# An attention and MLP kernel that runs by a written list: the list made anew

## The chip, the cores and the metric

The kernel runs on one core of a Trainium2 chip. The metric is the device time of one execution in microseconds (us). Before the change it is 630.63 us, the median of three runs (630.5 to 630.87).

## The reference

Everything is bf16 at the edges; S = 2048 rows, D = 512, 32 heads of 16 that share one key and one value (multi-query attention), F = 1792.

```
xn  = layernorm(x)
q   = (xn @ wq) per head;  k = xn @ wk;  v = xn @ wv
p   = softmax(q k^T / 4);  s = (p v, heads side by side) @ wo
g   = silu( silu(xn @ w1) @ w2 )
out = x + s * g
```

The 32 heads x 2048 x 2048 exponentials are the bulk of the work: 134 million of them.

## The kernel before

**Tiling.** The rows are cut into 4 chunks of 512 queries (`NQ`), the keys into 16 tiles of 128, the heads into 8 groups of 4. A *block* is one head, one key tile and one query chunk: 128 keys x 512 queries of scores, 2048 blocks in all. A *group* (32 of them, `gi`) is four heads of one chunk. TensorE makes a block's scores with a matmul of 32 rows of contraction in one of four row strips (`score`, L672); four strips run side by side. The products with V (`emit_quad`, L798) run in four column strips: four matmuls side by side are called a *quad*. Dense work (the MLP's two layers, the q projections and the output projection) runs in quads too (L433).

**Two ways to take an exponential.** ScalarE takes the exponential of two blocks at once from a psA buffer (two of 1024 columns, `exp_A`, L703) into one of 11 slots of `pa_sb`. VectorE takes a block from psD, psF or psO by adding a bias and writing int16, whose bits are a bf16 that approximates the exponential (`exp_D`, L743); two blocks that lie side by side in psD can be taken by one instruction of 1024 columns, a *pair*. GpSimd adds two constants to the finished four blocks of a key tile (`shift`, L768, `INT64_ADD`), so three weighted versions are summed by V's products: a VectorE block costs three V matmuls, a ScalarE block one. The versions lie in `ph_sb`, or in a part of `x_sb` that is free by then.

**Banks.** psA holds ScalarE's scores, psD two of VectorE's blocks, psF one dense job or a block, and psO the V products of the group that is open. At a group's end VectorE transposes psO (L911), later takes reciprocals (L920), normalises (L901, a `TENSOR_TENSOR` with two inputs in SBUF) and transposes back (L937). Only after the first transposition may the next group's V products begin. A *dense job* accumulates in a bank; ScalarE then takes a tanh (L1145) and VectorE the last step of silu (L1164), or VectorE alone evicts it (L1171, L1176).

**What sets the order.** After some 30 us, when the layer norm and the first projections are done, `follow` reads a string, `ORDER`, letter by letter, and issues each engine's instructions in that order; `finish` does the same with `TAIL`. Every engine then works in its own order, and waits are placed where data or banks demand them. The letters that matter here:

- `R0`/`R1`: a burst of two score blocks into psA; `e`: their exponential on ScalarE; `H`: such a burst of the last group's four first key tiles, which are done in three parts of the queries
- `o..` opens a key tile for VectorE, `f..` makes one of its blocks in a bank (0 and 1 psD, 2 psF, 3 psO), `x` evicts one block, `y` a pair
- `v`: one quad of V's products. Which blocks it takes (those that are ready first) is decided by a cost model of the engines in class `Sched`, which keeps estimated times for that purpose
- `J..b` opens a dense job in bank b, `d3` issues three of its quads, `t` its tanh, `E.` its eviction
- `1` to `4`: the four steps at a group's end
- in `TAIL`: `q`: V products of a part, `n`: a step of the part's normalisation, `P` and `r`: quads of the last output projection, `C`, `M`, `G`: evictions by ScalarE, VectorE or both, `X`, `Y`, `Z`/`z`: a tile of the output summed on TensorE, copied by ScalarE and stored, `A`/`B`: summed on VectorE and stored (the two cases name the queue that stores)

In `Sched.model`, a VectorE instruction with a pair as its cost is one with two tensors in SBUF; the model delays it behind GpSimd's additions that it finds in its way.

Of the kernel before, what the change touches and what calls it, by code (L numbers as in the profile page):

```python
# [35 lines left out]
class Sched:  # L36
# [64 lines left out]
    def model(self, eng, lane, cost, r):  # L101
        if lane:
            t = max(self.free[eng], r) + 0.05
            self.free[eng] = t + (0.86 if eng == "gp" else 0.5)
            return t + (cost or 2.25)
        if eng == "pe" and self.fine:
            mode, tiles, cols = cost or ("full", [None] * 4, 128)
            t = r
            for tile in tiles:
                end = self.pe_last + self.pe_len  # L110
                if mode != self.pe_mode:
                    t = max(t, end + (0.098 if mode == "row" else 0.1012))
                    self.pe_tiles, self.pe_pos = set(), 0
                elif tile is not None and tile not in self.pe_tiles:
                    t = max(t, self.pe_last + 0.0033)
                else:
                    self.pe_pos += 1
                    t = max(t, end + (0.003 if mode != "col" or self.pe_pos == 1 else -0.0075))
                    self.pe_tiles = set()
                self.pe_tiles.add(tile)  # L120
                self.pe_mode, self.pe_last, self.pe_len = mode, t, max(cols, 60) / 2400.0
            self.free[eng] = t
            return t + cols / 2400.0 + 0.2125
        if eng == "pe":
            mode, tiles, cols = cost or ("full", [None] * 4, 128)
            t = r
            for tile in tiles:
                if mode != self.pe_mode:
                    t = max(t, self.pe_last + self.pe_len + self.SWITCH)
                    self.pe_tiles = set()  # L130
                elif tile is not None and tile not in self.pe_tiles:
                    t = max(t, self.pe_last + 0.004)
                else:
                    t = max(t, self.pe_last + self.pe_len + 0.003)
                    self.pe_tiles = set()
                self.pe_tiles.add(tile)
                self.pe_mode, self.pe_last, self.pe_len = mode, t, max(cols, 60) / 2400.0
                self.pe_runs.append((t, t + self.pe_len))
            self.free[eng] = t
            return t + cols / 2400.0 + self.FLY + self.SEM  # L140
        if eng == "a" and self.fine:
            n = cost or 512
            t = max(r, self.free["a"], self.act_end - 0.428)
            self.free["a"] = t
            self.act_end = max(t + 0.1707 + n / 1200.0, self.act_end + 0.0632 + n / 1200.0)
            return self.act_end + 0.055
        if eng == "a":
            n = cost or 512
            t = max(r, self.free["a"], self.act_end - 0.428)
            self.free["a"] = t  # L150
            self.act_end = max(t + 0.274 + n / 1200.0, self.act_end + 0.0635 + n / 1200.0)
            return self.act_end + self.SEM
        t = max(r, self.free[eng] - (0.084 if eng == "v" else 0.0))
        if eng == "v" and isinstance(cost, tuple):

            t = max(r, self.free[eng] - 0.13)
            end = t + cost[0]
            for a, b in self.gp_runs[-6:]:
                if a < t - 0.1:
                    end = max(end, b + cost[0] - 0.13)  # L160
            self.tt_runs.append((t, end))
            self.free[eng] = end
            return end + (0.0565 if self.fine else self.SEM)
        end = t + (cost or 0.4)
        if eng == "gp" and cost and cost > 1.0:
            for a, b in self.tt_runs[-3:]:
                if a <= t + 0.1 and b > t:
                    end = max(end, b + 0.89)
            self.gp_runs.append((t, end))
        self.free[eng] = end - (0.02 if self.fine and eng == "gp" else 0.0)  # L170
        return end + (0.0565 if self.fine else self.SEM)
# [71 lines left out]
def bass_recurrent_scan__grouped_kv_mqa__dense_activation_silu__prompt_kernel(  # L243
# [76 lines left out]
        a=(0.3, 3.0, 0.65, 10, 1.2, 2.0, -4, 24, 0.2, 3, 3, 0.04, 9, 0.43, 0, 0.33, 0, 0),  # L320
# [7 lines left out]
    TAIL = "vvHvvHPvvvvvvvHHq0q0q0q0q1q1q1q1n0PPn1n0n1PPPq2q2q2n0n1n0q2PPr0r1n2C1n1n2n2G0Pr2Pn2PG2Pr3C3X1M1Y1A2A0M3Z1A3"  # L328
    ALPHA = "".join(chr(x) for x in range(35, 127) if x != 92) + "".join(chr(x) for x in range(192, 255))

    with ExitStack() as es:
# [1206 lines left out]
        while not followed:  # L1538
# [3 lines left out]
            if not followed and settled():  # L1542
# [3 lines left out]
                K.fine = True  # L1546
                follow(ORDER)
                followed = True
                continue
            t = max(now, min(K.pe_next("col"), K.pe_next("full")))  # L1550
# [14 lines left out]
            if more:  # L1565
# [4 lines left out]
                if TWIN and K.pe_mode == "row" and not front and release() <= K.pe_next("row") + 0.12:  # L1570
                    slots, t = 0, K.pe_next("row")
# [39 lines left out]
            else:  # L1611
                now = 0.0
        finish(TAIL)
        last = {}
# [36 lines left out]
```

## Time and profile before

| | |
|---|---|
| median of three runs | 630.63 us |
| the profiled execution: its own time / its span | 631.2 / 629.4 us |
| granted TensorE clock | 1.000 |
| ScalarE: exponentials of 128 x 1024 / tanh | 622 / 72 |
| VectorE: evictions of 512 / of 1024 columns (L743) | 708 / 48 |
| GpSimd: additions of 128 x 1024 (L768) | 402 |

The span runs from the first to the last instruction; the execution's own time is 1.8 us longer. In the groups of the page a mean duration counts from an instruction's start to its end, and instructions of one engine overlap a little, so the time from start to start is shorter than the mean. In a timeline, neighbours of one kind are merged into a row with their count. A `[0.23 <-PE psA L721]` behind a row is the idle time ahead of it and what ended that.

### The profile page before, as it was taken

How to read it: one execution, taken by the hardware profiler on the slowest of the kernel's cores; microseconds unless marked ns; L12 is line 12 of the kernel's file. 1: busy time of each engine (PE TensorE's matmuls, PEld its weight loads, DVE VectorE, ACT ScalarE, POOL GpSimd, SP SyncE). 2: the span in 40 equal slices, each digit the busy share in tenths (PEclk: the TensorE clock that was granted, in tenths of full speed). 3: DMA queues.
4: the chain of work that ended last, by engine and by line, in shares of the span. 5: the costliest groups of instructions: out<-in, count | busy, mean ns of one | idle time of the engine just before them, and what ended most of it. 6: DMA issues, size and time to landing. Idle time of an engine off the chain costs nothing.

```text
span 629.4 us, 18825 instructions
## 1 busy us (share of the span) xinstructions
PE 621.7 (99%) x8257; PEld 199.6 (32%) x8259; DVE 612.0 (97%) x1017; ACT 618.9 (98%) x714; POOL 443.5 (70%) x446
## 2 busy tenths in 40 slices
PE   8999999999999999999999999999999999999997
PEld 3422333333233333333332333323333233333333
DVE  7999999999999999999999999999999999999994
ACT  7999999999999999999999999999999999999996
POOL 5477665676766788676687767678775776787763
PEclk9999999999999999999999999999999999999999
DMA  6380000000000010000000000001000000000002
GB/s 178 126 287 1 2 2 2 2 1 3 1 3 2 2 18 11 10 2 2 1 3 2 1 3 1 2 11 18 10 2 2 2 2 1 2 3 1 11 11 51
DMA packets 10082, 12.50 MB, mean 20 GB/s; under 512 B 2288, under 2 KB 9456, under 8 KB 9968
## 3 DMA queue, kind: packets, MB, share of 16 engines
q1 hardware_dynamic: 7840, 9.34, 4.5%
q0 software_dynamic: 1728, 1.57, 2.2%
q8 instruction: 64, 1.05, 0.7%
q10 hardware_dynamic: 432, 0.39, 0.2%
q14 instruction: 18, 0.15, 0.1%
HBM read 8.95 MB, written 4.19 MB: 21 GB/s over the span
## 4 chain that ended last, share of the span: by engine, by line
PE 72%; ACT 24%; DVE 2%; DMA 1%; issue 0%; SPq 0%
PE psO L798 28%; PE psA L672 22%; ACT pa_sb L703 22%; PE psF L433 17%; PE psD L672 2%; ACT t_sb L1145 2%; DMA x_sb<-in_A_x_dram 1%; DVE ph_sb L743 0%; PE psF L672 0%; PE psD L536 0%; PE psD L505 0%; PE psA L721 0%; PE psD L562 0%; ACT xnT_sb L526 0%; DVE onb_sb L901 0%
## 5 line engine op out<-in xcount | busy, mean ns | idle before, releaser
L703 ACT ACTIVATE pa_sb<-psA 128x1024 bf16<-128x1024 f32 x622 | 583.5, 1058 | 2.5 <-PE psA L721 1.3
L768 POOL INT64_ADD ph_sb<-ph_sb x302 | 314.0, 1060 | 118.7 <-DVE ph_sb L743 118.3
L743 DVE TENSOR_SCALAR ph_sb<-psD 128x512 int16<-128x512 f32 (+1 forms) x462 | 320.6, 723 | 4.4 <-PE psD L672 3.5
L798 PE MATMUL psO<-ph_sb,vaug_sb 128*32 128x512 bf16 x1812 | 229.1, 384 | 0.0
L798 PE MATMUL psO<-pa_sb,vaug_sb 128*32 128x512 bf16 (+2 forms) x1276 | 205.5, 379 | 0.2 <-ACT pa_sb L703 0.2
L768 POOL INT64_ADD x_sb<-x_sb x100 | 104.1, 1057 | 41.6 <-DVE x_sb L743 41.4
L672 PE MATMUL psA<-qT_sb,kTb_sb 32*128 32x512 bf16 x616 | 118.8, 384 | 0.2 <-ACT pa_sb L703 0.2
L672 PE MATMUL psA<-qT_sb,kTa_sb 32*128 32x512 bf16 x612 | 116.5, 384 | 0.2
L672 PE MATMUL psD<-qT_sb,kTa_sb 32*128 32x512 bf16 x350 | 107.1, 384 | 0.5 <-DVE x_sb L743 0.5
L743 DVE TENSOR_SCALAR x_sb<-psD 128x512 int16<-128x512 f32 (+1 forms) x152 | 106.0, 717 | 0.9 <-PE psD L672 0.6
L798 PE MATMUL psO<-x_sb,vaug_sb 128*32 128x512 bf16 x600 | 105.1, 383 | 0.0
L672 PE MATMUL psD<-qT_sb,kTb_sb 32*128 32x512 bf16 x312 | 95.3, 384 | 0.0
L798 PEld LDWEIGHTS psO<-ph_sb,vaug_sb 128*32 128x32 bf16 x1812 | 59.1, 95 | 57.5 <-issue 34.2
L433 PE MATMUL psF<-w_sb,u_sb 128*32 128x512 bf16 x896 | 67.0, 383 | 0.0
L798 PEld LDWEIGHTS psO<-pa_sb,vaug_sb 128*32 128x32 bf16 x1276 | 52.5, 94 | 42.7 <-issue 31.1
L433 PE MATMUL psF<-xnT_sb,w_sb 128*32 128x512 bf16 x896 | 64.2, 382 | 0.0
L672 PEld LDWEIGHTS psA<-qT_sb,kTb_sb 32*128 32x128 bf16 x616 | 28.9, 91 | 109.3 <-ACT pa_sb L703 93.2
L672 PEld LDWEIGHTS psA<-qT_sb,kTa_sb 32*128 32x128 bf16 x612 | 28.7, 91 | 104.7 <-ACT pa_sb L703 78.5
L743 DVE TENSOR_SCALAR ph_sb<-psF 128x512 int16<-128x512 f32 x80 | 54.5, 681 | 0.1
L1145 ACT ACTIVATE t_sb<-psF 128x512 bf16<-128x512 f32 x72 | 45.2, 627 | 0.2 <-PE psF L433 0.2
L1164 DVE SCALAR_TENSOR_TENSOR u_sb<-t_sb,psF 128x512 bf16<-128x512 bf16 x56 | 37.9, 677 | 0.0
L798 PEld LDWEIGHTS psO<-x_sb,vaug_sb 128*32 128x32 bf16 x600 | 26.6, 95 | 20.1 <-issue 11.5
(120 smaller groups left out, 423.2 us busy)
## 6 DMA issues: line engine op xcount, KB each, us to landing
w_sb<-in_B_w_dram SPq DMA_DIRECT2D x2, 1792.0 KB, 12.1
x_sb<-in_A_x_dram SPq DMA_DIRECT2D x3, 512.0 KB, 5.8
out_dram<-ob_sb POOLq DMA_DIRECT2D x12, 128.0 KB, 3.1
wop_sb<-in_A_wo_dram SPq DMA_DIRECT2D x1, 512.0 KB, 4.4
wq_sb<-in_A_wq_dram SPq DMA_DIRECT2D x1, 384.0 KB, 5.8
out_dram<-ob_sb SPq DMA_DIRECT2D x3, 128.0 KB, 1.7
x_sb<-in_A_x_dram SPq DMA_DIRECT2D x2, 128.0 KB, 2.9
x_sb<-in_A_x_dram ACTq DMA_DIRECT2D x2, 128.0 KB, 3.1
```

Source lines behind the costliest of these rows:

```text
L433: r = e.matmul(bank[32 * i:32 * i + 32, :], lhsT=w, rhs=rhs, start=start, stop=stop, tile_position=(0, 32 * i), skip_group_check=True)
L672: return e.matmul(ap, lhsT=kT_sb[g % 2][32 * i:32 * i + 32, kt * P:(kt + 1) * P], rhs=qT_sb[32 * i:32 * i + 32, c % 2, g // 2, :], start=T ...
L703: d = op("a", lambda e: e.activation(pa_sb[:, sl, :], psA[k][:, :], ACT.Exp, scale=ESCALE), reads=["A%d" % k], writes=[("pa", sl)], cost=2 ...
L743: d = op("v", lambda e: e.tensor_scalar(ph_ap(0, sl, 512 * pos, 512 * pos + m), src, float(PH_ONE + PH_BIAS), 0.0, op0=ALU.add, op1=ALU.ma ...
L768: d = op("gp", lambda e, j=j: e.int64_add(ph_ap(j, sl, 0, 4 * NQ).bitcast(I64), ph_ap(0, sl, 0, 4 * NQ).bitcast(I64), PH_SHIFT[j] * 0x0001 ...
L798: r = e.matmul(psO[32 * i:32 * i + 32, cs], lhsT=vaug_sb[:, p["v"], p["kt"], DH * (gi % 2):DH * (gi % 2) + 32], rhs=p["ap"], start=s0, sto ...
L1145: d = op("a", lambda e: e.activation(t_sb[:, n % 2, :], bank_ap(b), ACT.Tanh, scale=0.5 if jb[0] == "h" else 0.25), reads=[b], writes=[("t ...
L1164: op("v", lambda e: e.scalar_tensor_tensor(out=dst, in0=t_sb[:, n % 2, :], scalar=1.0, in1=src, op0=ALU.add, op1=ALU.mult), reads=tk["read ...
```

## The change

The program's functions stay. `ORDER` and `TAIL` are replaced, and one line of the model that helps choose each quad's blocks:

```diff
@@ class Sched, model(): a VectorE instruction with two tensors @@
             for a, b in self.gp_runs[-6:]:
-                if a < t - 0.1:
+                if a < t + (0.15 if self.fine else -0.1):
                     end = max(end, b + cost[0] - 0.13)
...
-    ORDER = "R0xf11f01exJ$2d2R1xf10exd2R0E$o02f03evvR1xf10ev
...
+    ORDER = "R0xf11xf00eJ$2d3R1xf11xevd1R0E$o02f02evR1xf11eJ
...
-    TAIL = "vvHvvHPvvvvvvvHHq0q0q0q0q1q1q1q1n0PPn1n0n1PPPq2q2q2n0n1n0q2PPr0r1n2C1n1n2n2G0Pr2Pn2PG2Pr3C3X1M1Y1A2A0M3Z1A3"
+    TAIL = "q0vvHvHvvq0q0q0vvHHn0Pq1n0q1n0n0q1q1Pn1PPPr0n1n1Pr1q2q2q2q2G0PPPn2C1n1r2Pn2PM1n2A1C2Pn2r3X2B0M2G3Y2z2B3"
```

What the new list holds, counted letter by letter against the old one:

| | before | after |
|---|---|---|
| bursts into psA in `ORDER` (`R` and `H`) | 597 | 595 |
| key tiles for VectorE opened in `ORDER` | 199 | 200 |
| their evictions: single (`x`) / pairs (`y`) | 704 / 48 | 580 / 112 |
| V quads in `ORDER` / in `TAIL` (`v`) | 892 / 11 | 898 / 7 |
| dense jobs in psF / in psO | 99 / 0 | 77 / 22 |
| all exponentials on ScalarE | 622 | 620 |
| all additions on GpSimd | 402 | 404 |

**TensorE at the end of the second group.** Before: V's products (L798) of the group end, and a job of the MLP's first layer (`w_sb`, L433) follows in psF, then the next group's products. psA and psD rows are score bursts.

```order
L798 MATMUL psO<-pa_sb,vaug_sb 32x512 x2
L798 MATMUL psO<-ph_sb,vaug_sb 32x512 x6
L672 MATMUL psA<-qT_sb,kTa_sb 128x512 x2
L672 MATMUL psD<-qT_sb,kTa_sb 128x512
L433 MATMUL psF<-xnT_sb,w_sb 32x512 x16
L672 MATMUL psA<-qT_sb,kTa_sb 128x512 x2
L672 MATMUL psD<-qT_sb,kTa_sb 128x512
L798 MATMUL psO<-x_sb,vaug_sb 32x512 x2
L798 MATMUL psO<-pa_sb,vaug_sb 32x512
```

After:

```order
L798 MATMUL psO<-pa_sb,vaug_sb 32x512 x2
L798 MATMUL psO<-ph_sb,vaug_sb 32x512 x4
L798 MATMUL psO<-pa_sb,vaug_sb 32x512 x2
L433 MATMUL psF<-xnT_sb,w_sb 32x512 x4
L672 MATMUL psA<-qT_sb,kTa_sb 128x512 x2
L672 MATMUL psD<-qT_sb,kTa_sb 128x512 x2
L433 MATMUL psF<-xnT_sb,w_sb 32x512 x12
L672 MATMUL psA<-qT_sb,kTa_sb 128x512 x2
L433 MATMUL psO<-xnT_sb,w_sb 32x512 x16
L672 MATMUL psA<-qT_sb,kTa_sb 128x512 x2
L672 MATMUL psD<-qT_sb,kTa_sb 128x512 x2
L433 MATMUL psF<-xnT_sb,w_sb 32x512 x16
```

Here the next group's V products are put off; job after job runs in turn in psF and psO, six of them at this place, a job to nearly every burst.

**VectorE near the last group's beginning.** Evictions of scores (L743) ahead of the transposition that ends the group before the last. Before:

```order
L743 TENSOR_SCALAR ph_sb<-psF 128x512
L743 TENSOR_SCALAR ph_sb<-psD 128x512 x2
L743 TENSOR_SCALAR x_sb<-psF 128x512
L743 TENSOR_SCALAR x_sb<-psD 128x512 x2
L911 STREAM_TRANSPOSE otr_sb<-psO 128x16x32
```

After:

```order
L743 TENSOR_SCALAR ph_sb<-psD 128x1024
L743 TENSOR_SCALAR ph_sb<-psF 128x512
L743 TENSOR_SCALAR x_sb<-psD 128x1024
L743 TENSOR_SCALAR x_sb<-psF 128x512
L743 TENSOR_SCALAR x_sb<-psD 128x512
L743 TENSOR_SCALAR ph_sb<-psD 128x512
L911 STREAM_TRANSPOSE otr_sb<-psO 128x16x32
```

Two blocks in psD that were taken one by one are now taken together.

**TensorE ahead of the last exponentials.** L721 is a burst of the last group's parts; 32x256 and 32x128 are V products of a part, 32x512 those of whole tiles, `wop_sb` the last output projection. Before:

```order
L721 MATMUL psA<-qT_sb,kTb_sb 128x128 x8
L433 MATMUL psF<-wop_sb,xn_sb 32x512 x4
L798 MATMUL psO<-pa_sb,vaug_sb 32x512 x4
L798 MATMUL psO<-ph_sb,vaug_sb 32x512 x2
L798 MATMUL psO<-pa_sb,vaug_sb 32x512
L798 MATMUL psO<-ph_sb,vaug_sb 32x512
L798 MATMUL psO<-pa_sb,vaug_sb 32x512 x2
L798 MATMUL psO<-ph_sb,vaug_sb 32x512 x18
L721 MATMUL psA<-qT_sb,kTb_sb 128x128 x16
L798 MATMUL psO<-pa_sb,vaug_sb 32x256 x16
```

After:

```order
L721 MATMUL psA<-qT_sb,kTb_sb 128x128 x8
L798 MATMUL psO<-ph_sb,vaug_sb 32x512 x2
L798 MATMUL psO<-pa_sb,vaug_sb 32x512
L798 MATMUL psO<-ph_sb,vaug_sb 32x512
L721 MATMUL psA<-qT_sb,kTb_sb 128x128 x8
L798 MATMUL psO<-ph_sb,vaug_sb 32x512 x8
L798 MATMUL psO<-pa_sb,vaug_sb 32x256 x12
L798 MATMUL psO<-ph_sb,vaug_sb 32x512 x8
L721 MATMUL psA<-qT_sb,kTb_sb 128x128 x16
L433 MATMUL psF<-wop_sb,xn_sb 32x512 x4
L798 MATMUL psO<-pa_sb,vaug_sb 32x128 x16
```

The run of seven whole quads and a projection quad ahead of the last bursts has become one quad, a burst, and four whole quads with three of half the width; the first part's V products now stand ahead of the last bursts instead of behind them.

2 lines of the change are left out of this document (1 added, 1 removed).

## The prediction

> **What bounds the kernel now.** I read the page first: the busy shares, then the chain that ended last.
>
> ```profile
> span 629.4 us, 18825 instructions
> PE 621.7 (99%) x8257; PEld 199.6 (32%) x8259; DVE 612.0 (97%) x1017; ACT 618.9 (98%) x714; POOL 443.5 (70%) x446
> ...
> PE 72%; ACT 24%; DVE 2%; DMA 1%; issue 0%; SPq 0%
> ```
>
> Three engines are nearly full, so a share alone decides nothing. ScalarE's work is the plainest to count: the groups give the number of instructions, ScalarE's timeline the time from one start to the next (durations overlap: an exponential lasts 1.06).
>
> ```profile
> L703 ACT ACTIVATE pa_sb<-psA 128x1024 bf16<-128x1024 f32 x622 | 583.5, 1058 | 2.5 <-PE psA L721 1.3
> ...
> L1145 ACT ACTIVATE t_sb<-psF 128x512 bf16<-128x512 f32 x72 | 45.2, 627 | 0.2 <-PE psF L433 0.2
> ```
>
> ```profile
> 11.28 28.84 ACT L703 ACTIVATE pa_sb<-psA 128x1024 bf16<-128x1024 f32 x31 [0.59 <-PE psA L672]
> ...
> 499.57 13.94 ACT L703 ACTIVATE pa_sb<-psA 128x1024 bf16<-128x1024 f32 x15
> 513.32 0.68 ACT L1145 ACTIVATE t_sb<-psF 128x512 bf16<-128x512 f32 x1
> ...
> 516.62 0.62 ACT L1145 ACTIVATE t_sb<-psF 128x512 bf16<-128x512 f32 x1
> 517.11 3.79 ACT L703 ACTIVATE pa_sb<-psA 128x1024 bf16<-128x1024 f32 x4
> ...
> 614.85 4.81 ACT L703 ACTIVATE pa_sb<-psA 128x1024 bf16<-128x1024 f32 x5 [0.23 <-PE psA L721]
> 620.72 1.94 ACT L703 ACTIVATE pa_sb<-psA 128x1024 bf16<-128x1024 f32 x2 [1.06 <-PE psA L721]
> ```
>
> Fifteen exponentials take 513.32 - 499.57 = 13.75, 0.917 each; a tanh adds 517.11 - 516.62 = 0.49. From the first exponential (11.28) to the end of the last (620.72 + 1.94 = 622.66) pass 611.4 us. Without any stall 622 exponentials and 72 tanh take 621 x 0.917 + 1.06 + 72 x 0.49 = 605.8. So ScalarE bounds the kernel over this stretch and loses only 5.6 us in it; 11.3 lie ahead and 6.7 behind. The two idle times near the end, with 0.14 of overlap lost at each (1.058 - 0.917), are 0.37 + 1.20 = 1.57 of the 5.6.
>
> TensorE stands close behind. Starts of score bursts with two, three and one groups of column matmuls ("quads") between them:
>
> ```profile
> 595.95 0.39 PE L672 MATMUL psA<-qT_sb,kTa_sb 32*128 32x512 bf16 x2
> ...
> 596.82 0.39 PE L672 MATMUL psA<-qT_sb,kTa_sb 32*128 32x512 bf16 x2
> ...
> 597.90 0.39 PE L672 MATMUL psA<-qT_sb,kTa_sb 32*128 32x512 bf16 x2
> ...
> 598.56 0.39 PE L672 MATMUL psA<-qT_sb,kTa_sb 32*128 32x512 bf16 x2
> ```
>
> The steps are 0.87, 1.08 and 0.66: 0.215 a quad, and some 0.44 for the burst, of which two changes of mode are about 0.1 each. Two quads fit under one exponential (0.917), three don't.
>
> **The change part by part.** The profiled execution took 631.2 (1.8 beside its span), 0.57 above the median of 630.63. I sum the changes against its trace and take the sum off the median.
>
> *Fewer exponentials.* The new order has 620 on ScalarE, not 622: one more key tile of four blocks goes to VectorE. That is 2 x 0.917 = **-1.83**, in full while ScalarE bounds the stretch, nothing if TensorE takes it back.
>
> *VectorE.* Single evictions in the list fall from 704 to 580, pairs rise from 48 to 112.
>
> ```profile
> 442.63 0.67 DVE L1164 SCALAR_TENSOR_TENSOR u_sb<-t_sb,psF 128x512 bf16<-128x512 bf16 x1
> 443.23 1.21 DVE L743 TENSOR_SCALAR ph_sb<-psD 128x1024 int16<-128x1024 f32 x1
> 444.36 0.67 DVE L743 TENSOR_SCALAR ph_sb<-psF 128x512 int16<-128x512 f32 x1
> 444.96 1.29 DVE L743 TENSOR_SCALAR ph_sb<-psD 128x512 int16<-128x512 f32 x2
> ```
>
> Start to start a single is 0.60 (444.96 - 444.36), a pair 1.13 (444.36 - 443.23). The change is -124 x 0.60 + 64 x 1.13 = -2.1 us of VectorE, the four added blocks included. ScalarE's time falls by 1.83, so VectorE keeps pace: **0** on the path. Cover gone, a late eviction holds a score bank, up to 0.48 as in the TensorE row below.
>
> *Two-tensor work and GpSimd's additions.* The group normalisation (L901) comes 15 times in full size. Two of them, with the additions around them and what followed the slow one:
>
> ```profile
> 441.42 0.73 DVE L901 TENSOR_TENSOR onb_sb<-otr_sb,rcp_sb 128x512 bf16<-128x512 f32 x1
> ...
> 477.65 1.61 DVE L901 TENSOR_TENSOR onb_sb<-otr_sb,rcp_sb 128x512 bf16<-128x512 f32 x1
> ```
>
> ```profile
> 441.60 2.42 POOL L768 INT64_ADD x_sb<-x_sb  x2 [0.58 <-DVE x_sb L743]
> ...
> 476.62 2.05 POOL L768 INT64_ADD ph_sb<-ph_sb  x2 [1.15 <-DVE ph_sb L743]
> ```
>
> ```profile
> 479.89 0.39 PE L672 MATMUL psD<-qT_sb,kTa_sb 32*128 32x512 bf16 x1 [0.48 <-DVE x_sb L743]
> ```
>
> ```profile
> 479.45 2.11 ACT L703 ACTIVATE pa_sb<-psA 128x1024 bf16<-128x1024 f32 x2
> 481.83 1.02 ACT L703 ACTIVATE pa_sb<-psA 128x1024 bf16<-128x1024 f32 x1 [0.27 <-PE psD L672]
> 483.04 0.60 ACT L1145 ACTIVATE t_sb<-psF 128x512 bf16<-128x512 f32 x1 [0.18 <-PE psF L433]
> 483.54 7.43 ACT L703 ACTIVATE pa_sb<-psA 128x1024 bf16<-128x1024 f32 x8
> ```
>
> At 441.42 the normalisation started ahead of the addition and took 0.73; the pair of additions was stretched from 2.05 to 2.42. At 477.65 the second addition of the pair was just starting and the normalisation lasted 1.61. ScalarE then needed 483.54 - 479.45 = 4.09 for three exponentials and a tanh, 3.24 by the prices above: 0.85 lost. The new planning rule counts an addition that starts up to 0.15 after the normalisation as in its way. One loss in 15 goes: **-0.8**, bounds 0 and -0.85 here, and a loss again for each new collision (a rival).
>
> *Dense jobs in V's bank.* Of the 99 dense jobs 22 now accumulate in psO, between a group's transposition and the next group's first V product. Their quads, tanh and evictions are those they had in psF; only their place changes. V's products wait longer: between the two, the old list has 113 exponentials over 31 groups, the new 173, at most 9 at a place (7 before). Eleven pa slots cover it: in the new order the last V product that reads a slot always stands ahead of the score burst of the exponential that writes it again. A job's first matmul waits for the eviction of the job before in its bank, and behind it in TensorE's queue stand the next scores. The nearest rows:
>
> ```profile
> PEld psF L433 <- DVE u_sb L1164: 4.4, 21, 0.3
> ...
> PEld psD L672 <- DVE x_sb L743: 3.4, 9, 0.8
> ```
>
> That is 0.2 at most places, which an ordinary row shows between quads too: I take 0, with 22 x 0.3 = +6.6 as the far end and -1 (quads moved out of crowded steps) as the near one.
>
> *TensorE's balance.* A tile more on VectorE is 8 more V matmuls (two quads, +0.43) and two bursts less (-0.86 at most). Summed over the listed part by the prices above (quads 1448 to 1454, 597 to 595 bursts, 38 to 39 score blocks that can't run beside another, changes of mode), TensorE needs 565 before and 566 after, ScalarE 583 and 581: the spare falls from 18 to 15. The 3.2 us of stalls that are neither at the end nor the collision should grow with that: in proportion 3.2 x 18/15 = 3.8. I take **+0.5**, bounds -2 and +3 (all the lost spare).
>
> The Trainium skill (Perfetto Trace Analysis, Identifying the Most-Contended Engine) says to judge TensorE's headroom by the weight loads' busy share, not by the matmuls'. Here that is 32%, by which TensorE would have room, this term 0 and the sum 0.5 lower; the steps of 0.87 and 1.08 against 0.917 speak against it.
>
> *New end.* The old tail puts seven V quads in one run ahead of the last two score bursts:
>
> ```profile
> 619.10 1.25 PE L798 MATMUL psO<-ph_sb,vaug_sb 128*32 128x512 bf16 x18
> 620.28 0.42 PE L721 MATMUL psA<-qT_sb,kTb_sb 32*128 32x128 bf16 x16
> ```
>
> ScalarE's 1.06 of idleness (620.72) ends with that burst. The new tail has four V quads fewer (11 to 7), its longest run ahead of a burst is four V quads and three of half the width, and among the last eight bursts stand no dense matmuls any more (32 before). From the eighth burst before the end TensorE needs 7.3 us by the prices, ScalarE 8 x 0.917 = 7.3. Of the 1.57 I leave 0.3: **-1.27**, bounds 0 and -1.57.
>
> Behind the last exponential, rows of the old tail:
>
> ```profile
> 621.53 0.65 DVE L949 STREAM_TRANSPOSE otr_sb<-psO 128x256 f32<-128x256 f32 x2 [4.35 <-PE psO L798]
> ...
> 626.66 0.50 DVE L1473 TENSOR_TENSOR ob_sb<-wq_sb,x_sb 128x512 bf16<-128x512 bf16 x1
> ```
>
> The last part's V products now stand behind two of the output products, which wait for the first part's normalisation: some 0.4 later. VectorE's work behind them is one eviction shorter (0.6), since the first output tile is evicted ahead of that wait; the rest is the same kinds of instructions. The last store goes out from ScalarE's queue instead of SyncE's; both land alike:
>
> ```profile
> out_dram<-ob_sb SPq DMA_DIRECT2D x3, 128.0 KB, 1.7
> ...
> out_dram<-ob_sb ACTq DMA_DIRECT2D x1, 128.0 KB, 1.8
> ```
>
> The two nearly cancel, and the closing steps still wait for each other across three engines: I take **+0.2**, bounds -0.5 and +0.6.
>
> Sum: -1.83 - 0.8 + 0 + 0.5 - 1.27 + 0.2 = **-3.2**; 630.63 - 3.2 = 627.4.
>
> **The rivals.**
>
> *TensorE takes it back* (no change). The chain that ended last is TensorE's to 72%, and its work doesn't fall. Then the two exponentials bring nothing (+1.83), and the end moves no earlier than its V products (+0.8 of the 1.27): -3.2 + 2.6 = -0.6, 630.0. Against it: ScalarE's stalls are under 1% of its stretch.
>
> *The dense jobs hold up the scores* (slower). Each of the 22 jobs in psO starts a run of jobs that alternate between two banks, one per step, each with a tanh and an eviction that the job after next waits for. At 0.3 a job this is +6.6: 634.0. It decides from 3.2 / 22 = 0.15 a job, and is slower for certain above 0.2. For it: the runs leave VectorE an eviction more per step. Against it: over such a run VectorE's load (10.9 us in the first) stays under ScalarE's (11.2).
>
> *More collisions* (slower). If other normalisations fall behind an addition's start, each costs ScalarE 0.85; four undo the gain (-2.4 without the term above, plus 3 x 0.85), six give 632.5. For it: two more additions, and list and chip need differ by only 0.15. Against it: 14 of 15 went well before. The Trainium skill (SBUF — State Buffer, Who interferes with whom) has the rule: a VectorE instruction with two SBUF inputs and a GpSimd one that reads SBUF exclude each other, and whichever starts first keeps the other out. By that rule, the trace agrees: 0.73 ahead of an addition, 1.61 behind one.
>
> *Better still.* The new list also halves the scattered 3.2 and empties the end: -3.2 - 2.1 = -5.3, 625.3.
>
> **How the numbers follow.** Forecast case 0.55, better still 0.12, TensorE takes it back 0.15, dense jobs 0.12, collisions 0.06. The likeliest gives 627.4. The range reaches down to 625.2 (better still) and up to 631.6, past "takes it back" and into the lower part of the slower cases; some 0.2 lies outside, most of it above. A measurement of this kernel can tell about 0.2%, 1.3 us, from no change. Faster by more: 0.52 + 0.12 and half of "takes it back" = 0.72; within it 0.10; slower 0.18.
>
> **What would show it.** In the new profile: 620 exponentials still about 0.917 apart, from 11.3 to about 619.3; ScalarE's waits on psA (L721) under 0.5 in sum; no L901 of full size above 1 us; 6.5 to 7 us behind the last exponential. Wrong, if ScalarE's waits for scores grow to more than 3 us, if TensorE's waits for VectorE at psO's or psF's dense jobs do, or if the last exponential ends where it did.

## The result, and the profile after

The changed kernel takes **626.98 us** (median of 6 runs, 626.88 to 627.56) against 630.6 for the kernel before in the same series. The ratio is 0.9942, with a 95% interval of 0.993 to 0.9955. The forecast was 627.4, range 625.2 to 631.6.

The profiled execution after took 627.05 (span 625.2); the one before took 631.2. The page after, its busy line and the chain that ended last:

```profile
span 625.2 us, 18811 instructions
PE 618.2 (99%) x8265; PEld 197.4 (32%) x8267; DVE 610.4 (98%) x957; ACT 617.0 (99%) x712; POOL 441.1 (71%) x448
...
PE 65%; ACT 30%; DVE 2%; issue 1%; POOL 1%; DMA 0%; POOLq 0%
```

The shares of busy time decide nothing, as before. In the chain ScalarE's share has grown from 24% to 30%. Groups of the profile, each with one shape of operands: the exponentials, VectorE's pairs (the instructions of 1024 columns), the tanh that read psO, and the normalisations of full size:

```profile
L703 ACT ACTIVATE pa_sb<-psA 128x1024 bf16<-128x1024 f32 x620 | 581.9, 1063 | 1.2 <-PE psA L672 0.6 <-PE psA L721 0.3
L743 DVE TENSOR_SCALAR ph_sb<-psD 128x1024 int16<-128x1024 f32 x87 | 106.0, 1219 | 0.8 <-PE psD L672 0.5
L743 DVE TENSOR_SCALAR x_sb<-psD 128x1024 int16<-128x1024 f32 x25 | 30.5, 1220 | 0.0
L1145 ACT ACTIVATE t_sb<-psO 128x512 bf16<-128x512 f32 x19 | 12.1, 637 | 0.0
L901 DVE TENSOR_TENSOR onb_sb<-otr_sb,rcp_sb 128x512 bf16<-128x512 f32 x15 | 11.0, 733 | 0.0
```

All 15 normalisations of full size now run at some 733 ns (before: 789 in the mean, with the one of 1.61). ScalarE's timeline at the end:

```profile
610.94 5.71 ACT L703 ACTIVATE pa_sb<-psA 128x1024 bf16<-128x1024 f32 x6
616.94 1.94 ACT L703 ACTIVATE pa_sb<-psA 128x1024 bf16<-128x1024 f32 x2 [0.29 <-PE psA L721]
```

Of the two idle times before, 0.23 and 1.06, a single one of 0.29 is left. The last exponential ends at 618.88, and 6.36 lie behind it. And the waits of TensorE's weight loads at the dense jobs and at VectorE's scores (columns: sum, number, longest):

```profile
PEld psD L672 <- DVE ph_sb L743: 5.8, 20, 0.4
PEld psO L433 <- issue: 5.2, 23, 0.2
PEld psF L433 <- DVE u_sb L1164: 2.8, 12, 0.4
PEld psD L672 <- DVE x_sb L743: 1.7, 5, 0.4
PEld psO L433 <- DVE otr_sb L911: 1.1, 5, 0.2
PEld psO L433 <- DVE ph_sb L743: 0.9, 4, 0.2
PEld psO L433 <- DVE u_sb L1164: 0.5, 2, 0.3
```

At the 22 jobs in psO the weight loads wait 0.5, in two places, for the eviction of the job before; for the group's transposition and for evictions of scores they wait another 2.0, in nine places of at most 0.2. At psF the waits for the job before fell from 4.4 to 2.8. At psD the longest fell from 0.8 to 0.4, but the sum over both its rows rose from 6.8 to 7.5.

Where the time went, the two profiled executions side by side. *Stalls* are what ScalarE loses between its first and last exponential over 0.917 for each exponential and 0.49 for each tanh; they are added up from the ends of its instructions:

| us | before | after | difference |
|---|---|---|---|
| ahead of the first exponential | 11.28 | 10.80 | -0.48 |
| exponentials and tanh at their price | 605.8 | 603.9 | -1.83 |
| stall at the slow normalisation (477.65) | 0.85 | 0 | -0.85 |
| stalls after 610 | 1.62 | 0.39 | -1.23 |
| all other stalls | 3.1 | 3.8 | +0.6 |
| behind the last exponential | 6.70 | 6.36 | -0.34 |
| beside the span | 1.8 | 1.8 | 0 |

The first row isn't the change: the list begins only after some 30 us, and in the profiles of the runs below the first exponential starts anywhere from 10.65 to 11.60. The profiled execution before also lay 0.57 above its median, the one after only 0.07. The other rows give -3.65; the medians of the one series differ by 3.62, and 626.98 lies 3.65 under the 630.63 that the forecast started from.

### The profile page after: what moved, and what is told of

Its sections match the earlier page's. It is cut to its first block, busy times and chain, and to the rows that moved or that the text cites. A ratio compares the mean times of both kernels' runs of the same rounds, so it can differ in the third digit from the quotient of the medians.

```text
span 625.2 us, 18811 instructions
## 1 busy us (share of the span) xinstructions
PE 618.2 (99%) x8265; PEld 197.4 (32%) x8267; DVE 610.4 (98%) x957; ACT 617.0 (99%) x712; POOL 441.1 (71%) x448
## 3 DMA queue, kind: packets, MB, share of 16 engines
q0 software_dynamic: 1728, 1.57, 2.2%
## 4 chain that ended last, share of the span: by engine, by line
PE 65%; ACT 30%; DVE 2%; issue 1%; POOL 1%; DMA 0%; POOLq 0%
ACT pa_sb L703 27%; PE psO L798 26%; PE psA L672 21%; PE psF L433 12%; PE psO L433 2%; ACT t_sb L1145 2%; PE psD L672 2%; DVE ph_sb L743 1%; POOL ph_sb L768 0%; DMA x_sb<-in_A_x_dram 0%; PE psD L536 0%; PE psD L505 0%; PE psD L562 0%; ACT xnT_sb L526 0%; DVE stats_sb L453 0%
## 5 line engine op out<-in xcount | busy, mean ns | idle before, releaser
L743 DVE TENSOR_SCALAR ph_sb<-psD 128x512 int16<-128x512 f32 (+1 forms) x391 | 303.8, 799 | 2.6 <-PE psD L672 1.7
L798 PE MATMUL psO<-ph_sb,vaug_sb 128*32 128x512 bf16 x1836 | 228.2, 384 | 0.1
L798 PE MATMUL psO<-pa_sb,vaug_sb 128*32 128x512 bf16 (+2 forms) x1272 | 206.1, 378 | 0.0
L743 DVE TENSOR_SCALAR x_sb<-psD 128x512 int16<-128x512 f32 (+1 forms) x130 | 99.9, 784 | 0.9 <-PE psD L672 0.3
L798 PE MATMUL psO<-x_sb,vaug_sb 128*32 128x512 bf16 x588 | 98.2, 384 | 0.1
L672 PE MATMUL psD<-qT_sb,kTa_sb 32*128 32x512 bf16 x322 | 89.5, 384 | 0.0
L672 PE MATMUL psD<-qT_sb,kTb_sb 32*128 32x512 bf16 x311 | 83.1, 384 | 0.0
L743 DVE TENSOR_SCALAR ph_sb<-psF 128x512 int16<-128x512 f32 x115 | 78.1, 679 | 0.7 <-PE psA L721 0.6
L798 PEld LDWEIGHTS psO<-ph_sb,vaug_sb 128*32 128x32 bf16 x1836 | 58.2, 95 | 58.0 <-issue 37.2
L798 PEld LDWEIGHTS psO<-pa_sb,vaug_sb 128*32 128x32 bf16 x1272 | 52.1, 95 | 40.6 <-issue 30.4
L433 PE MATMUL psF<-w_sb,u_sb 128*32 128x512 bf16 x728 | 53.2, 383 | 0.0
L433 PE MATMUL psF<-xnT_sb,w_sb 128*32 128x512 bf16 x640 | 45.0, 382 | 0.0
L1145 ACT ACTIVATE t_sb<-psF 128x512 bf16<-128x512 f32 x53 | 33.3, 627 | 0.1
L672 PE MATMUL psF<-qT_sb,kTb_sb 32*128 32x512 bf16 x86 | 33.0, 384 | 0.0
L798 PEld LDWEIGHTS psO<-x_sb,vaug_sb 128*32 128x32 bf16 x588 | 24.4, 94 | 18.3 <-issue 12.4
```

What stands on the lines that cost most here:

```text
L433: r = e.matmul(bank[32 * i:32 * i + 32, :], lhsT=w, rhs=rhs, start=start, stop=stop, tile_position=(0, 32 * i), skip_group_check=True)
L672: return e.matmul(ap, lhsT=kT_sb[g % 2][32 * i:32 * i + 32, kt * P:(kt + 1) * P], rhs=qT_sb[32 * i:32 * i + 32, c % 2, g // 2, :], start=T ...
L743: d = op("v", lambda e: e.tensor_scalar(ph_ap(0, sl, 512 * pos, 512 * pos + m), src, float(PH_ONE + PH_BIAS), 0.0, op0=ALU.add, op1=ALU.ma ...
L798: r = e.matmul(psO[32 * i:32 * i + 32, cs], lhsT=vaug_sb[:, p["v"], p["kt"], DH * (gi % 2):DH * (gi % 2) + 32], rhs=p["ap"], start=s0, sto ...
L1145: d = op("a", lambda e: e.activation(t_sb[:, n % 2, :], bank_ap(b), ACT.Tanh, scale=0.5 if jb[0] == "h" else 0.25), reads=[b], writes=[("t ...
```

## The experiments

The kernel before took 630.7 to 630.8 beside all of these runs; 0.9942 of that is 627.1 to 627.2, with which the variants of the changed kernel are compared.

**The end of the old list, spread.** The run of seven V quads is split and four of them go behind a burst:

```diff
-    TAIL = "vvHvvHPvvvvvvvHHq0
+    TAIL = "vvHvvHPvvvHvvvvHq0
```

> The old list, with the last run of seven whole V quads cut: the last two score bursts stand three quads and four quads further, not together behind all seven. Theory (the burst is late because TensorE runs 1.5 us of quads ahead of it): the 1.06 us of idle time ahead of the last two exponentials goes, with 0.14 of lost overlap, so -1.2 us: 629.4. Rival (TensorE's work at the end is the bound, whatever its order): the V products and output products behind the bursts come later by as much, under -0.3: 630.3 to 630.6, with the idle time moved behind the last exponential.

Measured: 630.92, ratio 1.000 (0.9991 to 1.0009). Nothing gained. Its timeline at the end:

```profile
614.36 4.81 ACT L703 ACTIVATE pa_sb<-psA 128x1024 bf16<-128x1024 f32 x5 [0.23 <-PE psA L721]
619.37 1.02 ACT L703 ACTIVATE pa_sb<-psA 128x1024 bf16<-128x1024 f32 x1 [0.20 <-PE psA L721]
620.67 1.02 ACT L703 ACTIVATE pa_sb<-psA 128x1024 bf16<-128x1024 f32 x1 [0.28 <-PE psA L721]
```

The stall after 610 falls by 0.47 (1.62 to 1.15), and 7.24 instead of 6.70 lie behind the last exponential. What ScalarE gains comes back behind it.

**The end of the old list, with less work.** Of the last two dense jobs only the first and last quad of one, and the first of the other, are issued:

```diff
+            few = {("w", 11): (0, 3), ("w", 10): (0,)}.get(jb, items)
...
-                for m in items:
+                for m in [m for m in items if m in few]:
```

> The kernel before with 20 matmuls (5 quads, 1.08 us of TensorE) left out of the last two dense jobs, which stand among the last eight score bursts; all else, the run of seven V quads too, stays where it is. What the last two output tiles of those jobs hold is incomplete. Theory (the amount of TensorE work among the last eight bursts bounds the end): -0.8 to -1.1, 629.8, ratio 0.9985, and ScalarE's idle times ahead of its last exponentials fall from 0.23 and 1.06 to under 0.4 in sum. Rival (the run of V quads ahead of the last bursts makes the stall): no change, and the 1.06 stands.

Measured: 630.11, ratio 0.9988 (0.9979 to 0.9997), -0.68.

```profile
611.34 7.51 ACT L703 ACTIVATE pa_sb<-psA 128x1024 bf16<-128x1024 f32 x8
619.68 1.94 ACT L703 ACTIVATE pa_sb<-psA 128x1024 bf16<-128x1024 f32 x2 [0.83 <-PE psA L721]
```

The 0.23 is gone and the 1.06 is 0.83; the stall falls by 0.69, and this time 6.70 stay behind the last exponential. The gain is a little under the theory's 0.8 to 1.1, and the idle time of 0.83 is over its 0.4: the run of quads does leave a stall. But less work moved the time, and a spread of the same work didn't.

**Both edits of the end.**

> The kernel before with both edits of its end: the 20 matmuls of old_list_less_end left out (the last two output tiles of those jobs are incomplete) and the run of seven V quads split as in old_list_spread_end. Theory (less work and its spread together are what the new end has): ScalarE's idle time ahead of its last exponentials falls under 0.3 in sum, -1.2 to -1.4, 629.5. Rival (the V quads that are moved back come late behind the last exponential, as in old_list_spread_end): the sum stays near -0.7, 630.1, with 7.1 or more behind the last exponential.

Measured: 630.15, ratio 0.9991 (0.9982 to 1.0). The rival holds: the stall is down to 0.46, but 7.25 lie behind, and the spread adds nothing to the -0.68.

**The new end, spread further.** In the changed kernel one V quad goes from ahead of the last two bursts to between them:

```diff
-    TAIL = "q0vvHvHvvq0q0q0vvHHn0
+    TAIL = "q0vvHvHvvq0q0q0vHvHn0
```

> The changed kernel with one V quad moved from ahead of the last two score bursts to between them. Theory: the second-last burst comes 0.2 earlier, the 0.29 of idle time ahead of the last two exponentials falls to about 0.1, and the kernel takes 0.2 less than the changed one (627.2), 627.0. Rival (the quad and two more changes of mode come late for the last burst or behind it): no change or up to 0.3 slower.

Measured: 627.37, ratio 0.9947 (0.9934 to 0.9959): no gain. VectorE's first transposition of the last parts, after and in this run:

```profile
616.62 0.45 DVE L949 STREAM_TRANSPOSE otr_sb<-psO 128x256 f32<-128x256 f32 x1 [3.01 <-PE psO L798]
```

```profile
617.35 0.45 DVE L949 STREAM_TRANSPOSE otr_sb<-psO 128x256 f32<-128x256 f32 x1 [3.46 <-PE psO L798]
```

The exponentials started 0.25 later in this profile (11.05); the other 0.48 is real. The transposition waits for the quad that was put back, and the close begins later by as much: the stall after 610 falls from 0.39 to 0.18, and 6.89 lie behind the last exponential.

**The new close, with less on VectorE.** Two output tiles get x added on TensorE and are written by ScalarE:

```diff
-G0PPPn2C1n1r2Pn2PM1n2A1C2Pn2r3X2B0M2G3Y2z2B3
+G0PPPX0Y0n2C1z0n1r2Pn2PM1n2X1C2Pn2r3Y1X2z1M2G3Y2z2B3
```

> The changed kernel with a new close: two of the four output tiles get x added on TensorE (two products with the identity each) and are written by ScalarE, in place of two additions on VectorE (L1473, 0.33 and 0.31 start to start). Theory (behind the last exponential VectorE runs without a pause from 619.44 to 622.60, so its work sets the end): the last addition ends 0.3 to 0.6 earlier, the kernel takes 626.7 against the changed one's 627.2. Rival (the chain from the last V products over the last normalisation and the last output product sets the end, and ScalarE and TensorE lie on it too): within 0.2, or slower by up to 0.5.

Measured: 627.93, ratio 0.9955 (0.9941 to 0.9968), 0.85 above the changed kernel. Two rows of it:

```profile
621.93 0.59 ACT L1453 ACTIVATE wq_sb<-psD 128x512 bf16<-128x512 f32 x1
...
622.55 0.42 DVE L1455 TENSOR_TENSOR wq_sb<-wq_sb,tmp_sb 128x512 bf16<-128x512 bf16 x1 [1.02 <-ACT wq_sb L1453]
```

VectorE now stands idle for 1.02: the tile that it needs is copied by ScalarE, which has the added copy ahead of it. The rival's direction came true, with more than its 0.5. VectorE's unbroken row of work in the close held work that had time; it was not what set the end.

The seven kernels' ends beside each other:

| us | stalls after 610 | behind the last exponential | sum | time |
|---|---|---|---|---|
| before | 1.62 | 6.70 | 8.32 | 630.6 to 630.8 |
| old, spread | 1.15 | 7.24 | 8.39 | 630.92 |
| old, less work | 0.93 | 6.70 | 7.63 | 630.11 |
| old, both | 0.46 | 7.25 | 7.71 | 630.15 |
| changed | 0.39 | 6.36 | 6.75 | 627.1 |
| changed, spread further | 0.18 | 6.89 | 7.07 | 627.37 |
| changed, close on ScalarE | 0.39 | 7.23 | 7.62 | 627.93 |

Within the old list's four rows and within the changed list's three the time follows the sum, not the stall alone. The two lists can't be set against each other this way, since they differ by more than the end.

**The slow normalisation, moved.** In the old list the twelfth `3` goes behind the second eviction after it:

```diff
-vEpvR03f03f12eJt2xd4vR1xf00teR0
+vEpvR0f03f12eJt2xd4vR1x3f00teR0
```

> The kernel before with one thing moved: the normalisation that took 1.61 us stands two evictions later, behind the end of the pair of additions. Theory: it takes 0.73, ScalarE's loss of 0.85 there is gone, 630.0 against 630.8 (ratio 0.9987). Rival (VectorE's next work or the scattered stalls take it back): no change, and ScalarE loses as much within the next 5 us. Third: the move makes a new collision with the next pair of additions: slower by up to 0.85.

Measured: 630.12, ratio 0.9987 (0.9978 to 0.9996), -0.67. VectorE at the place, and the group:

```profile
477.40 1.29 DVE L743 TENSOR_SCALAR x_sb<-psD 128x512 int16<-128x512 f32 x2 [0.23 <-PE psD L672]
478.61 0.74 DVE L901 TENSOR_TENSOR onb_sb<-otr_sb,rcp_sb 128x512 bf16<-128x512 f32 x1
```

```profile
L901 DVE TENSOR_TENSOR onb_sb<-otr_sb,rcp_sb 128x512 bf16<-128x512 f32 x15 | 11.0, 732 | 0.0
```

1.61 has become 0.74, and the stalls between 400 and 500 us fall from 1.40 to 0.84. The theory holds for the normalisation and in direction for the time. Its price was too high: of the 0.85 only some 0.57 goes, by the stalls, and the rest stays in the same stretch without a collision.

**Collisions added.** In the changed kernel 13 of the 15 normalisations are put one eviction behind the one that completes a key tile, so that they meet the pair of additions which that tile sets off. The first of them:

```diff
-d1R03f13o03f02teJ*2E)d4R1xteJ+3xd3
+d1R0f13o03f02teJ*2E)d4R1xteJ+3x3d3
```

> The new list, with 13 of the full-size normalisations (L901) moved one eviction behind the one that completes a key tile, so that each starts while GpSimd's pair of additions for that tile runs. Theory (the one that starts second waits, and the wait reaches ScalarE as it did at 477.65 in the kernel before): each takes 1.6 us or more, not 0.73, and costs ScalarE 0.85 or more, so 13 x 0.85 = +11 us, 638. Rival (VectorE's spare and the banks absorb it): the normalisations are long all the same, but the time rises by under 2 us, to 629.

Measured: 642.56, ratio 1.0181 (1.0165 to 1.0196), +15.4. One of the places, and the group:

```profile
415.53 2.48 POOL L768 INT64_ADD x_sb<-x_sb  x2 [2.17 <-DVE x_sb L743]
415.93 1.23 DVE L901 TENSOR_TENSOR onb_sb<-otr_sb,rcp_sb 128x512 bf16<-128x512 f32 x1
```

```profile
L901 DVE TENSOR_TENSOR onb_sb<-otr_sb,rcp_sb 128x512 bf16<-128x512 f32 x15 | 16.6, 1105 | 0.0
```

A normalisation that falls into the first addition waits for that one alone and takes about 1.2; the second addition is then kept out in its turn (the pair takes 2.48, not 2.05). Eleven of the 13 take about 1.2 and one 0.94; one, at 146.95, was not slowed (0.73). The normalisations themselves took 5.6 more in all; ScalarE's stalls are up by 14.9. Some 4.5 of these come from one place at 208 us, an event that the next experiment has too and explains; the rest, 10.4, is 0.8 for each of the 13. In the 8 us from the start of each of the 12 slow ones ScalarE loses 0.4 to 1.1, against at most 0.26 in the changed kernel.

**The pairs undone.** Every `y` of the new list becomes `xx`.

> The new list, with each of its 112 paired evictions written as two single ones in the same place. VectorE has 112 x (2 x 0.60 - 1.13) = 7.8 us more to do, against a spare of 8.4 us over the listed part. Theory (VectorE keeps pace because of its spare): under +1.5 us, 627 to 628.5; the first of the two banks even comes free sooner. Rival (VectorE is as much a bound as ScalarE, and the pairs paid for the two exponentials): most of the 7.8, 632 to 635, with TensorE waiting for evictions.

Measured: 637.02, ratio 1.0095 (1.0073 to 1.0117), +9.9. Over half is one event, after which ScalarE loses 5.5:

```profile
202.63 1.16 POOL L1151 DMA_DIRECT2D out_dram<-ob_sb  x1
203.64 2.27 POOL L768 INT64_ADD ph_sb<-ph_sb  x2
...
205.96 0.61 PE L798 MATMUL psO<-ph_sb,vaug_sb 128*32 128x512 bf16 x2 [3.24 <-POOL ph_sb L768]
```

With other estimated times the model picked other blocks for a V quad: one whose addition stood on GpSimd behind the issue of a DMA. TensorE waited 3.24 with the scores queued behind it. The experiment mixes two things, so a second one keeps every choice of blocks as it was: each pair is issued as two instructions in its old place.

```diff
+            def evict(e):
+                for h in range(len(blks)):
+                    r = e.tensor_scalar(ph_ap(0, sl, 512 * (pos + h), 512 * (pos + h) + 512), src[:, 512 * h:512 * h + 512],
...
+            d = op("v", evict,
```

> The changed kernel with each of its 112 pairs issued as two single evictions at the same place, both banks released as before, so that V's quads stand where they stood. It adds 112 x (2 x 0.60 - 1.13) = 7.8 us to VectorE. Theory (VectorE is nearly as full as ScalarE, so the added time reaches the end in good part): +4 to +6 over the changed kernel's 627.2, 631 to 633, in many ScalarE stalls of 0.1 to 0.3 and none of over 1 us. Rival (VectorE had spare, and the 9.9 of pairs_undone came from V quads that were placed anew): under +2, below 629.

Measured: 631.89, ratio 1.0018 (1.0009 to 1.0027), +4.8 for 7.8 of VectorE. The chain that ended last:

```profile
PE 80%; ACT 9%; DVE 8%; issue 1%; POOL 1%; DMA 0%; POOLq 0%
```

ScalarE's share falls from 30% to 9%, VectorE's rises from 2% to 8%. ScalarE's stalls rise by 4.9 in all, spread over the run with no single one above 0.5: many late banks, each of which holds up a burst. The theory holds; VectorE has little to spare.

**Four tiles back to ScalarE.** In the changed kernel four key tiles go from VectorE to ScalarE (628 exponentials, 8 V quads less). One piece:

```diff
-vvR1xo01f00f11evyR0f23evvvR0xf02evxo03f10f21R1xevvvR0x
+vvR1xevR0eR1eR0evvR0evo03f10f21R1xevvR0x
```

> The new list, with four key tiles (in four different groups) given back from VectorE to ScalarE: 628 exponentials, not 620, 16 evictions and 8 additions less, 8 V quads less, 8 score bursts more. Theory (ScalarE is the bound and every exponential counts in full): 8 x 0.917 = +7.3 us, 634.3. Rival (TensorE is the bound): 8 bursts at 0.43 less 8 quads at 0.215 = +1.7 us, 628.7, with ScalarE's stalls shrinking. VectorE as the bound would give a shorter time, to -9 us.

Measured: 635.5, ratio 1.0072 (1.0057 to 1.0088), +8.3, or 2.1 for each tile. ScalarE's count alone gives 8 x 0.917 = 7.3. Its two exponentials a tile count in full. The other 1.0 are stalls; the stretch from 300 to 400 us alone holds 1.2 more than in the changed kernel.

A normalisation fell behind an addition's start in this run without being put there. ScalarE's exponentials of that time, and the two engines that met:

```profile
104.79 6.56 ACT L703 ACTIVATE pa_sb<-psA 128x1024 bf16<-128x1024 f32 x7
...
106.26 2.48 POOL L768 INT64_ADD ph_sb<-ph_sb  x2
106.39 1.49 DVE L901 TENSOR_TENSOR onb_sb<-otr_sb,rcp_sb 128x512 bf16<-128x512 f32 x1
```

It took 1.49, and the seven exponentials beside it ran without a stall (6 x 0.917 + 1.06 = 6.56): a collision doesn't always reach ScalarE. One of the four tiles was taken from VectorE at this very place, four evictions of it, so the row doesn't price a collision where VectorE is full.

**TensorE loaded.** The changed kernel with 32 quads of zeros:

```diff
+                    if nv[gi] == 10 and pend[gi]:
+                        op("pe", lambda e: columns(e, psO, zero_sb[:, 0:P], zero_sb[:, :], False, False), ...
```

> The changed kernel with one quad of zeros more (4 matmuls into psO that add nothing to the result) behind the tenth V quad of each of 32 rounds of V: 32 x 0.215 = 6.9 us of TensorE, spread over the run, all else where it was. Theory (my forecast's rule for TensorE: 15 us of spare, scattered stalls in inverse proportion): 3.8 x 15 / (15 - 6.9) = 7.0 us of stalls, +3.2 over the changed kernel's 627.2, 630.4. Rival 1 (TensorE bounds it everywhere): +6.9, 634.1. Rival 2 (TensorE has spare outside the end): under +1.

Measured: 633.15, ratio 1.0038 (1.0024 to 1.0051), +6.1 for 6.9 of TensorE. The chain:

```profile
PE 83%; ACT 11%; DVE 3%; issue 1%; POOL 1%; DMA 0%; POOLq 0%; SPq 0%
```

That lies near the first rival's +6.9, far from my rule's +3.2: here a quad that the list didn't plan for costs nearly its whole time.

**One bank for the dense jobs.** Of the 22 jobs in psO 12 go to psF, and the evictions are moved ahead of the next job:

```diff
-R0texJ)32d2E(d1d1R03
+R0texE(J)22d2d1d1R03
```

> The changed kernel with 12 of the 22 dense jobs of psO put into psF, where the dense job before must be evicted first, so that jobs follow each other in one bank and VectorE evicts them earlier. Theory (the second bank is what lets two jobs alternate without a wait): each such job's first matmul waits for the tanh and the eviction before it, 0.6 to 1.2 us, with the scores queued behind: +7 to +14 over 627.2, 634 to 641. Rival (the place makes no difference, as my forecast of 0 for the move had it): under +2.

Measured: 663.67, ratio 1.0529 (1.0506 to 1.0551), +36.5, far beyond the theory's +7 to +14. An early place:

```profile
59.77 0.60 ACT L1145 ACTIVATE t_sb<-psF 128x512 bf16<-128x512 f32 x1 [0.96 <-PE psF L433]
...
60.40 0.69 DVE L1164 SCALAR_TENSOR_TENSOR u_sb<-t_sb,psF 128x512 bf16<-128x512 bf16 x1 [0.74 <-ACT t_sb L1145]
...
61.14 1.05 PE L433 MATMUL psF<-xnT_sb,w_sb 128*32 128x512 bf16 x16 [1.10 <-DVE u_sb L1164]
```

Here the three engines wait for each other in a ring: TensorE 1.10 for the eviction, VectorE 0.74 for the tanh, ScalarE 0.96 for the job. In the whole run matmuls in psF wait 25.0 us for such evictions, at 21 places. So jobs that follow each other at every burst need the second bank. The moved evictions also change what VectorE does first, so the 36.5 are not the price of the bank alone.

## Why the prediction was right

- *Fewer exponentials, -1.83*: right. Each of the 620 still costs 0.917, and four tiles given back cost 8.3 where eight exponentials are 7.3. The rival "TensorE takes it back" falls: by TensorE's work alone the four tiles would have cost 1.7.
- *VectorE, 0*: right, but it rests on the pairs. Undone in place they cost 4.8 for 112; by that rate the 64 new pairs, which spare 4.5 us of VectorE (64 x 0.07), hide some 2.8 us, an estimate.
- *Two-tensor work, -0.8*: right in direction and within its bounds, a little too large: the move alone gives -0.67 in time and -0.57 in stalls. I had put the whole 0.85 lost from 479.45 to 483.54 down to the collision. The reason given was partly wrong too. The new planning rule has no part in it: with the old line in its place the changed program has the same instructions in the same order on every engine. The new list itself has the normalisation elsewhere. None of the rival's new collisions arose. Its price of 0.85 for each is about right where they were put in (0.8 in the mean), but no constant: the one that arose with four tiles given back cost nothing, at a place where VectorE had four evictions less. The rule of the Trainium skill (SBUF — State Buffer, Who interferes with whom) that whoever starts first keeps the other out agrees with the row of the run with collisions added: 1.23 behind a first addition, and the second addition then held up.
- *Dense jobs in V's bank, 0*: right by the trace. The waits of psO's jobs for the job before are 0.5 in sum, and ScalarE shows no wait for them. No run tries the place alone; the one-bank run moves evictions too.
- *TensorE's balance, +0.5*: the other stalls grew by 0.6 (by 0.3, if the collision is priced at 0.57), but the way to it failed, so the hit is luck. I took 15 us of spare as usable, with stalls in inverse proportion; 6.9 of load gave +6.1, not +3.2. My explanation is that TensorE's spare lies in steps in which no work can be put, and that the new list gets by because its two bursts less and two quads more were planned together; no run shows this. The weight loads' share, one of the two measures by which the Trainium skill (Perfetto Trace Analysis, Identifying the Most-Contended Engine) judges TensorE's headroom, was 32% after as before, and 32% in the loaded run; the +6.1 speaks against that rule here.
- *New end, -1.27*: stalls after 610 fell by 1.23, but of the two causes given only one held. The first was the run of seven V quads; spreading that run brought nothing (ratio 1.000). The second was the amount of TensorE work from the eighth burst on (7.3 against ScalarE's 7.3 in the new list); leaving out 1.08 of that work brought 0.68. What the new end has less is work: among the last eight bursts stood 22 quads (13 of V, 9 dense), and now stand 14 of V and four of half the width, which in the old list came behind the last burst. Counted up to the point at which both the last burst and those four are through, that is 8 quads less, 1.72 us. Stalls and close together fell by 1.57; by the rate of the experiment (0.68 for 1.08) it would be 1.1, an estimate, and the other 0.5 was not told apart.
- *Behind the last exponential, +0.2*: wrong in sign, -0.34. The term that failed is the 0.4 by which the last part's V products were to come later. VectorE's transposition of that part, before and after:

```profile
623.17 0.32 DVE L949 STREAM_TRANSPOSE otr_sb<-psO 128x128 f32<-128x128 f32 x1 [0.23 <-PE psO L798]
```

```profile
619.44 0.32 DVE L949 STREAM_TRANSPOSE otr_sb<-psO 128x128 f32<-128x128 f32 x1
```

  It starts 0.51 behind the end of the last exponential before (622.66) and 0.56 after (618.88), 0.05 later instead of 0.4. The output products ahead of it wait for the first part's normalisation, and that now begins earlier: its transposition starts 2.26 ahead of the last exponential's end (616.62), not 1.13 (621.53). I had counted the close as its own stage. It belongs with the end's stalls, since the first part's normalisation waits for the same queue of TensorE work that the last bursts wait in.

Sum forecast -3.2, measured -3.65: -1.83, -0.85, -1.23, +0.6 and -0.34. No version tried beats the changed kernel; how much a list could still win in its 3.8 us of scattered stalls stays open.

## What to carry to other kernels

When three engines are each nearly full and their order is fixed, one engine's idle time at a place is a symptom: judge an edit by the work it takes from the queue that everything waits in, and sum the stall with what lies behind it, or the gain may only move. Don't take a spare that is counted over a whole stretch as room for added work: here 6.9 us of it cost 6.1. And make each probe with every later choice frozen, since here a changed choice of blocks alone held TensorE up for 3.24 us at one place.

## What the hardware showed that I hadn't expected

- A normalisation with two SBUF inputs that meets GpSimd's pair of additions pays by the moment of its start: 1.61 at the boundary of the two (it lost to the second one), 1.49 when it starts 0.13 behind the first one's start, 1.23 at 0.40 behind it, and 0.73 otherwise. With 1.06 for an addition, each of the three ends some 0.6 behind the end of the addition that it met; this is an estimate, since the rows show the additions in pairs.
- In the run with one bank TensorE stood idle more often, and its granted clock was lower in some stretches of 50 us. The columns are the stretch and its length, the busy time and instructions of TensorE, its weight loads, VectorE, ScalarE and GpSimd, then the granted clock, the DMA share and GB/s:

```profile
400.00:450.00 50.00, 45.91 (x560) 13.01 (x556) 41.81 (x63) 42.25 (x48) 31.66 (x32) 0.90 0.08 9
500.00:550.00 50.00, 50.00 (x682) 15.38 (x678) 49.74 (x72) 49.93 (x58) 36.35 (x36) 1.00 0.01 2
```

  The clock did not follow the busy time alone: it was 0.93 in a stretch with 43.82 us busy and 0.93 in one with 46.85. The lower clock may be a part of the +36.5; it wasn't told apart.
